# A gated MLP after sliding-window attention: the kept z pair's seven operand pieces made by GpSimd, through its own DMA queue

## The chip, the cores and the metric

The kernel runs on one core of a Trainium2 chip. The time is that of the device, in microseconds: 1127.86 us before the change, the median of three runs (1126.88 to 1131.13). Engines are called by the profile's names: PE is TensorE's matmul and PEld its weight load, DVE is VectorE, ACT is ScalarE, POOL is GpSimd, SP is SyncE, and a q behind the name (SPq) is the engine's queue of instructions, where DMAs are issued.

## The reference, cut to what matters

One block of a transformer on 2048 rows of 640 columns: a sliding-window attention (32 heads of 20, window 256) with its residual, and a gated MLP. The change lies in the second part:

```python
z  = gelu(layernorm(h) @ w_in)                                  # 2048 x 1728
z1 = z[..., :864]
z2 = layernorm(z[..., 864:])                                    # 2048 x 864
g  = einsum("ts,sf->tf", w_sp, z2) + b_sp[:, None]              # 2048 x 2048 by 2048 x 864
h2 = h + (z1 * g) @ w_out
```

The product with `w_sp` is the gate.

## The kernel before, in words

All matrix products are done in float32 pieces: each operand is split into a rounded high part (hi) and the rest (lo = raw - hi), and three products (hi hi, hi lo, lo hi) are summed in PSUM.

The gate cuts the 16 row tiles of z2 into pairs (tile k and tile k + 4, or k + 8 and k + 12), and uses a scheme of seven block products in place of eight. For each pair, the two tiles of 864 columns are four blocks of 432 columns (b11, b12 from one tile, b21, b22 from the other), and the right operand of the seven products are the seven pieces B11, T1 = b12 - b11, T2 = b22 - T1, B22, T3 = b22 - b12, B21 and T4 = b21 - T2, each as hi and lo. They lie in `zc[k]`, seven tiles of 128 x 2 x 432 for each of four k (named ze and zl in the profile). The sum over s is cut in halves. The opening half (`first_gate(p)`, p = 0 to 7) uses the z2 tiles 0 to 7 and stores its partial result to DRAM (`g_d`). Then `z2_pair` makes the other pairs, whose pieces overwrite `zc`, and `second_gate(p)` does the second half, loads the partial result, gates, and projects by `w_out`.

The first pair of the second half (tiles 8 and 12, `z2_pair(12, 8, 12, 0, True)`) is made ahead, before the opening half, when the four sets of `zc` are still full. This is the kept z pair. In the kernel before, DVE forms the raw pieces in place in the pair's two row buffers, with four subtractions between the stores: SP stores b11, b21, b22, T1, T3, T2, T4 to `z2_d`, each 128 x 432 (216 KB). Then `staged_pieces` takes one piece after the other through one SBUF tile, `stage` (128 x 2 x 432): SP loads the raw piece into `stage[:, 1]`, ACT rounds it into `stage[:, 0]` (hi), DVE subtracts in place to get lo, and SP stores both halves to `zp_d[m]` (432 KB). When PE has used a set of `zc[0]` for the last time, SP loads the finished pieces from `zp_d` (`ze<-zp_d`).

Each engine executes its instructions in order. In the attention part the order on PE, DVE and ACT is as written (`manual_schedule`). From there on, a scheduler of the tile framework puts the instructions of all engines in order, by its own simulated times, from the program order of the steps: `steps` is the list of products, and `at(n, f)` puts f in front of step n. `run(n)` emits both. A gate pair is seven steps of 12 matmuls of 128 x 432 (L1086).

For the gate's left operand, SP loads two tiles of `w_sp` per pair p into `fx` (two halves that take turns, L1036). ACT and DVE make seven pieces from them in `aw`: `copy` (ACT, L719) for hi, `minus` (DVE, L713) for lo and for the block sums, the one with two inputs in `tmp1` and `fx`. The posts of each step take PSUM to the row buffers: `copy` on ACT or `plus` on DVE (`row<-g`). There are four row buffers of 128 x 864. SP stores each finished row to `g_d` (L1099, L1100). A `copy` or `minus` has the helper's line (L719, L713) whatever it works on, so the tile names tell them apart.

Two more users of the same places: `e1["h"][0]`, the home of four raw tiles of `w_out` (`load_wout`, L1193, `stage<-w_out_in`) and later of h, is `stage` too. And POOL has nothing to do in the opening half of the gate.

## Time and profile before

| | |
|---|---|
| median of three runs | 1127.86 us (1126.88 to 1131.13) |
| profiled execution: its time, its span | 1126.43 us, 1124.6 us |
| mean granted TensorE clock in it | 0.997 |
| PE busy | 1090.6 us, 97% of the span |
| DVE, ACT, POOL busy | 719.1, 576.7, 307.4 us |
| opening half of the gate on PE | 697.85 to 838.10 us, 672 matmuls |
| staging of the kept pair (`stage` as its tile) | first load issued at 709.04 us, last store at 760.02 us |

The profile is one execution. Its views are: busy time by engine, groups of instructions by line and tile (count, busy time, mean length in ns, idle time of the engine just before them and what ended it), waits by who waited for whom, the timeline, the chain of work that ended last, and the table by stretches (busy time and count on each engine between two moments). Moments are counted from the start of the span.

### The profile page before, as it was taken

How to read it: one execution, taken by the hardware profiler on the slowest of the kernel's cores; microseconds unless marked ns; L12 is line 12 of the kernel's file. 1: busy time of each engine (PE TensorE's matmuls, PEld its weight loads, DVE VectorE, ACT ScalarE, POOL GpSimd, SP SyncE). 2: the span in 40 equal slices, each digit the busy share in tenths (PEclk: the TensorE clock that was granted, in tenths of full speed). 3: DMA queues.
4: the chain of work that ended last, by engine and by line, in shares of the span. 5: the costliest groups of instructions: out<-in, count | busy, mean ns of one | idle time of the engine just before them, and what ended most of it. 6: DMA issues, size and time to landing. Idle time of an engine off the chain costs nothing.

```text
span 1124.6 us, 27720 instructions
## 1 busy us (share of the span) xinstructions
PE 1090.6 (97%) x10667; PEld 976.9 (87%) x10667; DVE 719.1 (64%) x2049; ACT 576.7 (51%) x1228; POOL 307.4 (27%) x454
## 2 busy tenths in 40 slices
PE   8999999999999999989899999999999999999998
PEld 7998877668888776879899999889989899999998
DVE  6541113889999997687376578555547884556442
ACT  4334333259999999566666567333336521222210
POOL 3114444457777778311100254000002000000000
PEclk9999999999999999999999999999999999999999
DMA  7212665656666653688564511654371563344331
GB/s 258 77 31 100 174 213 175 207 199 200 205 214 205 203 166 122 199 277 271 208 194 161 166 54 40 200 179 166 124 256 40 177 211 118 125 148 147 99 95 59
DMA packets 88036, 181.78 MB, mean 162 GB/s; under 512 B 11536, under 2 KB 49680, under 8 KB 83984
## 3 DMA queue, kind: packets, MB, share of 16 engines
q1 hardware_dynamic: 85600, 174.76, 48.2%
q10 hardware_dynamic: 2304, 5.24, 1.2%
q8 instruction: 84, 1.38, 0.5%
q14 instruction: 48, 0.39, 0.1%
HBM read 118.65 MB, written 62.51 MB: 161 GB/s over the span
## 4 chain that ended last, share of the span: by engine, by line
PE 71%; DMA 9%; DVE 7%; issue 4%; POOL 3%; ACT 3%; SPq 2%; POOLq 0%; ACTq 0%; DVEq 0%
PE g L1086 18%; PE out_ps L1125 8%; PE pv L431 6%; PE bank L403 5%; PE bank L337 5%; PE zb L950 4%; PE zx L898 3%; PE zv L898 2%; PE qk L521 2%; PE qk L523 2%; PE qk L522 2%; DMA fx<-hn_d 2%; PE zy L898 2%; POOL sg L540 2%; DMA fx<-wsp_in 1%
## 5 line engine op out<-in xcount | busy, mean ns | idle before, releaser
L406 ACT ACTIVATE pt<-bank 128x384 f32<-128x384 f32 (+2 forms) x512 | 200.3, 492 | 11.8 <-PE bank L403 8.1
L719 ACT ACTIVATE aw<-fx 128x512 fp32r<-128x512 f32 (+2 forms) x160 | 93.0, 594 | 158.9 <-PE g L1086 91.0
L1086 PE MATMUL g<-zl,aw 128*128 128x432 f32 x768 | 171.9, 359 | 1.3 <-ACT zl L719 1.2
L349 DVE CUSTOM_DVE_ANT_0 junk<-bank,strip 128x288 bf16<-128x288 f32 x392 | 157.6, 454 | 2.6 <-PE bank L337 1.1
L1086 PEld LDWEIGHTS g<-zl,aw 128*128 128x128 f32 x768 | 143.6, 188 | 8.7 <-ACT zl L719 1.9
L1086 PE MATMUL g<-ze,aw 128*128 128x432 f32 x576 | 135.8, 363 | 6.0 <-DVE row L713 4.2
L431 PE MATMUL pv<-pt,v_sb 128*32 128x192 f32 (+3 forms) x1984 | 126.5, 321 | 2.5 <-POOL pt L411 1.8
L1086 PEld LDWEIGHTS g<-ze,aw 128*128 128x128 f32 x576 | 106.3, 188 | 14.6 <-ACT aw L719 5.5
L713 DVE TENSOR_TENSOR aw<-fx,aw 128x512 fp32r<-128x512 f32 (+2 forms) x152 | 96.9, 646 | 27.7 <-ACT aw L719 26.0
L403 PE MATMUL bank<-slot 123*32 123x288 bf16 (+5 forms) x1536 | 105.9, 280 | 3.1 <-issue 2.2
L1125 PE MATMUL out_ps<-wout,y_sp 128*128 128x320 f32 (+1 forms) x630 | 96.5, 309 | 0.4 <-ACT y_sp L135 0.4
L408 POOL TENSOR_SCALAR_AFFINE_SELECT pt<-pt 128x512 f32<-128x512 f32 x128 | 82.7, 647 | 47.1 <-ACT pt L406 46.1
L950 PE MATMUL zb<-win,aw 128*128 128x432 f32 x480 | 95.5, 359 | 0.0
L1125 PEld LDWEIGHTS out_ps<-wout,y_sp 128*128 128x128 f32 (+1 forms) x630 | 94.3, 188 | 1.2 <-ACT y_sp L135 0.7
L950 PEld LDWEIGHTS zb<-win,aw 128*128 128x128 f32 x480 | 89.9, 188 | 4.9 <-DVE aw L713 0.4
L337 PE MATMUL bank<-slot 120*32 120x288 bf16 (+2 forms) x1264 | 89.0, 283 | 1.1 <-DVE mcol L349 1.0
L537 DVE TENSOR_TENSOR rest<-qk,sg 128x512 f32<-128x512 f32 x40 | 27.7, 691 | 86.2 <-ACT sg L535 82.0
L411 POOL TENSOR_SCALAR_AFFINE_SELECT pt<-pt 128x512 f32<-128x512 f32 x112 | 73.7, 658 | 0.0
L713 POOL TENSOR_TENSOR aw<-fx,aw 128x640 fp32r<-128x640 f32 x8 | 13.5, 1692 | 217.2 <-ACT aw L719 217.2
L403 PEld LDWEIGHTS <-slot 123*32 123x32 bf16 x1536 | 52.7, 96 | 18.3 <-issue 7.4
L431 PEld LDWEIGHTS pv<-pt,v_sb 128*32 128x32 f32 x1984 | 59.5, 110 | 7.5 <-POOL pt L411 3.8
L540 POOL TENSOR_TENSOR sg<-rest,sg 128x512 bf16<-128x512 f32 x40 | 46.6, 1166 | 69.2 <-ACT sg L539 63.5
(193 smaller groups left out, 2172.7 us busy)
## 6 DMA issues: line engine op xcount, KB each, us to landing
fx<-wsp_in SPq DMA_DIRECT2D x32, 512.0 KB
slot<-qk_d SPq DMA_DIRECT2D x72, 200.0 KB
qk_d<-sg SPq DMA_DIRECT2D x32, 384.0 KB
slot<-qk_d SPq DMA_DIRECT2D x72, 160.0 KB
fx<-hn_d SPq DMA_DIRECT2D x32, 320.0 KB
o_d<-ot SPq DMA_DIRECT2D x64, 128.0 KB
z_d<-row SPq DMA_DIRECT2D x16, 432.0 KB
g_d<-row SPq DMA_DIRECT2D x16, 432.0 KB
```

Of the source, the lines that this page charges most:

```text
L337: nc.tensor.matmul(ps[32 * j:32 * j + 32, :n], part(st, half, 120, 0, hh, q0, 32), part(st, half, 120, 1, hh, lo + skip * j, n), start=Tru ...
L349: nc.vector.tensor_tensor_reduce(out=junk[:, :n], in0=ps[:, :n], in1=keep, scale=1.0, scalar=NEG, op0=OP.add, op1=OP.max, accum_out=m_cols ...
L403: nc.tensor.matmul(ps[32 * i:32 * i + 32, b:e], part(st, half, 123, 1, hh, k0, 32), part(st, half, 123, 0, hh, kb * P + b, e - b), start=T ...
L406: nc.scalar.activation(pt[:, hh, :n], ps[:, :n], AF.Exp, scale=SCALE)
L408: nc.gpsimd.affine_select(out=pt[:, :, :P], in_=pt[:, :, :P], pattern=[[0, 4], [1, P]], base=0, channel_multiplier=-1, compare_op=OP.is_ge ...
L431: nc.tensor.matmul(ps[32 * hh:32 * hh + 32, a - 512 * c:b - 512 * c], v_sb[:, kb, v0:v0 + 32], pt[:, hh, a - kb * P:b - kb * P], start=fir ...
L713: (eng or nc.vector).tensor_tensor(out=out, in0=a, in1=b, op=op)
L719: nc.scalar.activation(out, a, AF.Copy)
L898: nc.tensor.matmul(ps, a[x], b[:, y], start=start and m + x + y == 0, stop=stop and m == n - 1 and x == 1, skip_group_check=True)
L950: nc.tensor.matmul(b[0][:, :HF], a[t][:, x, kk], win2[0][:, y, kk, h * HF:(h + 1) * HF], start=kk + x + y == 0, stop=kk == KD - 1 and x == 1)
L1086: nc.tensor.matmul(ps, w[m][x][:, k], zc[k][m][:, y], start=start and k + x + y == 0, stop=stop and k == 3 and x == 1, skip_group_check=True)
L1125: nc.tensor.matmul(ps[j][:, :HD], src[:w, a, k, :], e1["wout"][:w, b, k, j * HD:(j + 1) * HD], start=(k == 0 and a + b == 0), stop=(k == K ...
```

## The change

The two tiles of the kept pair are stored whole and once (`z2_d` is now two tiles of 128 x 864), right after they are normalized. The four subtractions on DVE in the row buffers are gone. Everything after that is GpSimd's: for each piece it loads the block (and, for T1 to T4, the block or kept sum that is subtracted, into the place of hi), subtracts, stores the sums T1 and T2 - which T2 and T4 need - to a new DRAM tensor `t_d`, makes hi with a `tensor_copy` and lo with a subtraction, and stores both to `zp_d`. All these DMAs are issued in GpSimd's own queue. The pieces come in another order (B11, T1, B21, T2, B22, T3, T4); the loads of `zp_d` into `zc` stay on SP, and in their old order.

```diff
-    z2_d = dram.tile([7, P, HF], F32, name="z2_d")
+    z2_d = dram.tile([2, P, FH], F32, name="z2_d")
+    t_d = dram.tile([2, P, HF], F32, name="t_d")
...
-            b11, b12, b21, b22 = blocks
-
-            def keep(m, raw):
-                nc.sync.dma_start(z2_d[m], raw)
-
-            at(n0 + 4, lambda: keep(B11, b11))
-            at(n0 + 5, lambda: (keep(B21, b21), keep(B22, b22)))
-            at(n0 + 7, lambda: (minus(b11, b12, b11), minus(b12, b22, b12)))
-            at(n0 + 8, lambda: (keep(T1, b11), keep(T3, b12)))
-            at(n0 + 9, lambda: minus(b11, b22, b11))
-            at(n0 + 10, lambda: (keep(T2, b11), minus(b21, b21, b11)))
-            at(n0 + 11, lambda: keep(T4, b21))
+            for t in range(2):
+                at(n0 + 4 + t, lambda t=t: nc.sync.dma_start(z2_d[t], z[t]))
             return
...
     def staged_pieces(n0, n1):
-        raw = stage.bitcast(F32)[:, 1]
+        hi, raw = (stage.bitcast(F32)[:, k] for k in range(2))
+        eng = nc.gpsimd
+        b11, b12, b21, b22 = (z2_d[t, :, h * HF:(h + 1) * HF] for t in range(2) for h in range(2))
+
+        def piece(m, src, less=None, keep=None):
+            eng.dma_start(raw, src)
+            if less is not None:
+                eng.dma_start(hi, less)
+                minus(raw, raw, hi, eng)
+            if keep is not None:
+                eng.dma_start(keep, raw)
+            eng.tensor_copy(out=stage[:, 0], in_=raw)
+            minus(stage[:, 1], raw, hi, eng)
+            eng.dma_start(zp_d[m], stage.bitcast(F32))
+
+        for i, p in enumerate(((B11, b11), (T1, b12, b11, t_d[0]), (B21, b21), (T2, b22, t_d[0], t_d[1]), (B22, b22),
+                               (T3, b22, b12), (T4, b21, t_d[1]))):
+            at(n0 + 6 * i, lambda p=p: piece(*p))
         for i, m in enumerate((B11, T1, T2, B22, T3, B21, T4)):
-            n = n0 + 6 * i
-            at(n, lambda m=m: nc.sync.dma_start(raw, z2_d[m]))
-            at(n + 2, lambda: copy(stage[:, 0], raw))
-            at(n + 3, lambda: minus(stage[:, 1], raw, stage[:, 0].bitcast(F32)))
-            at(n + 4, lambda m=m: nc.sync.dma_start(zp_d[m], stage.bitcast(F32)))
             at(n1 + i + 1, lambda m=m: nc.sync.dma_start(zc[0][m].bitcast(F32), zp_d[m]))
...
-    staged_pieces(len(steps) + 8, len(steps) + 49)
+    staged_pieces(len(steps) + 4, len(steps) + 49)
```

What the scheduler makes of it is seen at three places. The first is POOL's order at the start of the gate's opening half (`mvz` is the column of layernorm statistics; `z_d` stands for `z2_d`, since numbers are cut from names). Before, the next work behind the last `mvz` belongs to the z pairs after the opening half:

```order
L976 TENSOR_TENSOR mvz_0_11692<-mvz_0_11692,half 128x1
L976 TENSOR_TENSOR mvz_1_11738<-mvz_1_11738,half 128x1
L713 TENSOR_TENSOR aw<-fx,aw 128x640 x2
```

With the change, the seven pieces stand between these two, of which the first two (B11, then T1) are:

```order
L977 TENSOR_TENSOR mvz_1_11739<-mvz_1_11739,half 128x1
L1004 DMA stage<-z_d 128x432
L1010 CAST stage<-stage 128x432
L714 TENSOR_TENSOR stage<-stage 128x432
L1012 DMA zp_d<-stage 128x864
L1004 DMA stage<-z_d 128x432
L1006 DMA stage<-z_d 128x432
L714 TENSOR_TENSOR stage<-stage 128x432
L1009 DMA t_d<-stage 128x432
L1010 CAST stage<-stage 128x432
L714 TENSOR_TENSOR stage<-stage 128x432
L1012 DMA zp_d<-stage 128x864
```

In all, POOL gains 20 DMAs, 7 casts and 11 subtractions there. The second place is ACT's order in the first pairs of the gate (`row<-g` takes a product out of PSUM, `aw<-fx` is a left operand's hi). Before:

```order
L719 ACTIVATE row_9611<-g_0_0_0_11767 128x432
L719 ACTIVATE stage<-stage 128x432
L719 ACTIVATE aw<-fx 128x512
L719 ACTIVATE row_9609<-g_1_0_0_11894 128x432
L719 ACTIVATE stage<-stage 128x432
L719 ACTIVATE aw<-fx 128x512
L719 ACTIVATE aw<-tmp_9614 128x512
L719 ACTIVATE row_9610<-g_1_1_1_11913 128x432
L719 ACTIVATE aw<-fx 128x512
L719 ACTIVATE stage<-stage 128x432
L719 ACTIVATE aw<-fx 128x512 x2
```

and now:

```order
L720 ACTIVATE row_9612<-g_0_0_0_11768 128x432
L720 ACTIVATE aw<-fx 128x512
L720 ACTIVATE row_9610<-g_1_0_0_11890 128x432
L720 ACTIVATE aw<-fx 128x512
L720 ACTIVATE aw<-tmp_9615 128x512
L720 ACTIVATE row_9611<-g_1_1_1_11908 128x432
L720 ACTIVATE aw<-fx 128x512 x3
```

The rest of ACT's order is the same without the `stage` rows, and DVE's is likewise: the seven `stage<-stage` subtractions and the four in the row buffers are out, the others keep their order (but for one neighbouring pair). On PE the same matmuls stand in the same order, but for a few groups of one to three in pairs 1 to 4, where the scheduler lets the products of two pairs alternate. The third place is SP's queue, at the first load of `w_out` into `stage`. Before, it stood behind the last `zp_d` store and the fifth `g_d` store of the opening half:

```order
L1011 DMA stage<-z_d 128x432
L1014 DMA zp_d<-stage 128x864
L1099 DMA g_d<-row_9611 128x864
L1193 DMA stage<-w_out_in 128x640
L1036 DMA fx<-wsp_in 128x1024
L1100 DMA g_d<-row_9612 128x864
```

and now it stands behind the tenth:

```order
L1103 DMA g_d<-row_9613 128x864
L1039 DMA fx<-wsp_in 128x1024
L1102 DMA g_d<-row_9612 128x864
L1196 DMA stage<-w_out_in 128x640
L1039 DMA fx<-wsp_in 128x1024
L1103 DMA g_d<-row_9611 128x864
```

Behind it there are the same stores and `w_sp` loads as before, and then the `ze<-zp_d` loads. From SP's queue 19 DMAs are gone: seven stores of raw pieces have become two of whole tiles, and seven loads and seven stores of `stage` are POOL's now.

## The prediction

> **What bounds the kernel now.** I read the busy times first: PE is busy for 97% of the span, so only PE's idle time can be won. Then I asked the stretch table for the gate's products alone (columns: stretch, its length, busy time and count on PE and on PEld, granted clock, share and rate of DMA).
>
> ```profile
> PE 1090.6 (97%) x10667; PEld 976.9 (87%) x10667; DVE 719.1 (64%) x2049; ACT 576.7 (51%) x1228; POOL 307.4 (27%) x454
> 697.85:760.62 62.77, 58.20 (x288) 53.33 (x288) 1.00 0.51 171
> 760.62:829.60 68.98, 68.65 (x348) 65.25 (x348) 1.00 0.49 157
> 829.60:838.10 8.50, 7.61 (x36) 6.61 (x36) 1.00 0.96 306
> ```
>
> The opening half is cut where the staging of the kept pair ends. Behind it, 348 matmuls take 68.98 us with 0.33 idle: 68.65 / 348 = 0.197 us each. At that pace the 288 matmuls ahead of it need 56.8 us; they took 62.77. So 6.0 us are lost while the staging runs. The clock is 1.00 in both, so it isn't that. The timeline of PE names the places (start, duration, what; in brackets the idle time before it and who ended it):
>
> ```profile
> 715.88 0.87 PE L1086 MATMUL g<-ze,aw 128*128 128x432 f32 x3 [1.37 <-DVE row L713]
> 726.25 0.66 PE L1086 MATMUL g<-ze,aw 128*128 128x432 f32 x2 [1.05 <-ACT aw L719]
> 753.36 0.86 PE L1086 MATMUL g<-ze,aw 128*128 128x432 f32 x3 [0.20 <-DVE row L713]
> 760.66 1.41 PE L1086 MATMUL g<-ze,aw 128*128 128x432 f32 x6 [1.93 <-DVE row L713]
> ```
>
> They sum to 4.55 us; the other 1.4 or so is the slow restart (3 matmuls in 0.86 us instead of 0.59) and some shorter gaps. Who is late shows on ACT and DVE:
>
> ```profile
> 716.28 0.53 ACT L719 ACTIVATE row<-g 128x432 f32<-128x432 f32 x1 [3.44 <-DMA z_d<-row]
> 725.11 0.56 ACT L719 ACTIVATE stage<-stage 128x432 fp32r<-128x432 f32 x1 [4.35 <-DMA stage<-z_d]
> 758.79 0.56 ACT L719 ACTIVATE stage<-stage 128x432 fp32r<-128x432 f32 x1 [4.76 <-DMA stage<-z_d]
> 759.39 0.61 DVE L713 TENSOR_TENSOR stage<-stage 128x432 fp32r<-128x432 f32 x1 [3.25 <-ACT stage L719]
> 759.91 0.60 DVE L713 TENSOR_TENSOR row<-g,row 128x432 f32<-128x432 f32 x1
> ```
>
> ACT reaches a hi of the kept pair, waits 4 to 5 us for its load, and DVE then waits for ACT; the PSUM sum of 759.91, which PE needs at 760.66, stands behind both. The stall of 726.25 is an `aw` hi behind the same wait on ACT. At 716.28 ACT waits for a row buffer that is being stored as a raw piece, while DVE makes T1, T3 and T2 in these buffers. From 700 to 770 us the groups are (count, busy time, mean ns, idle time ahead), and the third row is one of the four subtractions in the row buffers:
>
> ```profile
> L719 ACT ACTIVATE stage<-stage 128x432 fp32r<-128x432 f32 x7 | 4.0, 564 | 20.5 <-DMA stage<-z_d 20.5
> L713 DVE TENSOR_TENSOR stage<-stage 128x432 fp32r<-128x432 f32 x7 | 4.2, 605 | 12.2 <-ACT stage L719 12.2
> 713.58 0.61 DVE L713 TENSOR_TENSOR row<-row,row 128x432 f32<-128x432 f32 x1
> ```
>
> **The change part by part.** *Removed from ACT and DVE.* ACT loses 4.0 us of work and 20.5 of waiting, DVE 4.2 + 4 x 0.6 = 6.6 us and 12.2 of waiting. All three causes of the four stalls go with it, since the two tiles are stored at once and free their rows. Without them the 288 matmuls should run as the next 348 do, whose ACT and DVE have the same gate work: minus 6.0 us on PE's path. What follows the opening half hangs on PE and shifts with it; the 8.50 - 36 x 0.197 = 1.4 us lost behind 829.60 have no `stage` in them and stay.
>
> *SP* issues 19 fewer DMAs and has no `zp_d` store to wait with. SP's own time is not on the path, so this counts nothing by itself; the cover is that the `w_sp` loads are in time behind 760.62 as well, under the same rules.
>
> *Added to POOL.* Its work costs nothing while it ends before POOL or its results are wanted: POOL idled 133.63 us up to 838.87. The results are wanted earlier, by the `ze<-zp_d` loads and, ahead of these, by `stage<-w_out_in`, which now follows the tenth `g_d` store:
>
> ```profile
> 838.87 1.57 POOL L713 TENSOR_TENSOR aw<-fx,aw 128x640 fp32r<-128x640 f32 x1 [133.63 <-ACT aw L719]
> 704.67 4.35 DMA z_d<-row
> 709.04 2.69 DMA stage<-z_d
> 712.98 2.41 DMA zp_d<-stage
> 721.87 3.13 DMA stage<-z_d
> 794.33 0.33 SPq L1099 DMA_DIRECT2D g_d<-row  x1
> 797.58 0.33 SPq L1036 DMA_DIRECT2D fx<-wsp_in  x1
> 801.35 0.69 DVE L713 TENSOR_TENSOR fx<-fx 128x512 f32<-128x512 f32 x1 [1.43 <-DMA fx<-wsp_in]
> 801.35 1.15 ACT L719 ACTIVATE aw<-fx 128x512 fp32r<-128x512 f32 x2 [1.74 <-DMA fx<-wsp_in]
> ```
>
> The four DMA rows are from the chain of waits, the others from the timeline. Shifted by 6.0, SP comes to that load at 788.3, and the `w_sp` load behind it is wanted at 791.6. If POOL is not done then, the `w_sp` load is late, and ACT and DVE start on it the moment it lands: there is next to no slack. So POOL's chain has from about 709.3 (the whole tile's store takes the 4.35 us of the half tile's, a little more with twice the bytes) to 791.6: **82 us**.
>
> How long is it? Within a piece every step waits for the one before, since raw and lo share a place. Prices from rows (the slowest load of the staging, and POOL's groups over the whole span):
>
> ```profile
> 729.08 0.32 SPq L1011 DMA_DIRECT2D stage<-z_d  x1
> 734.76 0.56 ACT L719 ACTIVATE stage<-stage 128x432 fp32r<-128x432 f32 x1 [1.83 <-DMA stage<-z_d]
> L713 POOL TENSOR_TENSOR row<-row,row 128x432 f32<-128x432 f32 x6 | 8.1, 1344 | 7.2 <-DVE row L713 3.4 <-ACT row L982 1.5 <-DVE zl L713 1.1
> L408 POOL TENSOR_SCALAR_AFFINE_SELECT pt<-pt 128x512 f32<-128x512 f32 x128 | 82.7, 647 | 47.1 <-ACT pt L406 46.1
> L360 POOL CAST m<-mr 128x40 bf16<-128x40 f32 (+1 forms) x16 | 4.0, 249 | 1.0
> L976 POOL TENSOR_TENSOR mvz<-mvz,half 128x1 f32<-128x1 f32 x16 | 10.1, 631 | 44.6 <-DVE mvz L975 44.6
> ```
>
> A subtraction is 1.3 us. A cast of 432 columns lies between 0.25 (40 columns) and 1.34; I take 0.6, from the one-input operation on 512 columns. A load of 216 KB is 2.7 us and a 432 KB store 2.4 when SP issues them. No row shows a DMA issued by GpSimd. Below, it costs what SP's does (0.3 us of issue, inside these times). Above, each takes the slowest that this stage shows, 4.35 us for a store and 5.7 for a load (issued at 729.08, used at 734.76). I add 0.6 us per DMA, because even the smallest POOL instruction takes 0.63. Then a plain piece (B11, B21, B22) is 3.3 + 0.6 + 1.3 + 3.0 = 8.2 us; T3 and T4 have a second load issued behind the first (0.6) and a subtraction more, 10.1; T1 and T2 also wait for the kept sum's store (3.0, of which 0.6 lie under the cast), 12.5. In all 3 x 8.2 + 2 x 10.1 + 2 x 12.5 = 70 us, ending at 779. The lower bound is 58 (20 x 0.6 less), ending at 767; the upper, with 7 loads 2.4 dearer, 9 stores 1.4 dearer and 7 casts 0.7 dearer, 104, ending at 813. I take 70: 12 us to spare, or 0.6 us more for each of the 20 DMAs.
>
> The Trainium skill ("DMA: Bandwidth & Descriptors", Specifications) gives the first byte of a DMA from GpSimd as about 1 us, against 0.6 from SP. By that the surcharge is 0.4 us per DMA, and the estimate of the chain 66 us instead of 70: the same verdict.
>
> *POOL beside DVE.* What POOL does at the same time as DVE is not free for DVE. Before the gate, between 600 and 700 us, where POOL works on the z pairs, DVE's subtractions are longer than in the gate:
>
> ```profile
> L713 DVE TENSOR_TENSOR ze<-row,ze 128x432 fp32r<-128x432 f32 x9 | 8.1, 906 | 1.8 <-ACT ze L719 1.8
> L713 DVE TENSOR_TENSOR zl<-row,zl 128x432 fp32r<-128x432 f32 x11 | 8.5, 795 | 0.1
> L713 DVE TENSOR_TENSOR row<-g,row 128x432 f32<-128x432 f32 x9 | 5.3, 599 | 0.0
> 657.03 1.55 POOL L713 TENSOR_TENSOR row<-row,row 128x432 f32<-128x432 f32 x1 [1.53 <-ACT row L982]
> 658.55 1.93 POOL L713 TENSOR_TENSOR aw<-fx,aw 128x640 fp32r<-128x640 f32 x1
> 658.07 2.87 DVE L713 TENSOR_TENSOR ze<-row,ze 128x432 fp32r<-128x432 f32 x2 [0.47 <-ACT ze L719]
> 660.00:680.00 20.00, 20.00 (x104) 19.04 (x103) 15.07 (x32) 13.42 (x23) 13.30 (x13) 1.00 0.20 60
> ```
>
> The first two rows are from that stretch, the third from the gate between 700 and 770. Two DVE subtractions beside POOL took 2.87 us instead of 1.2. By the first two groups, 20 operations were stretched by 9 x 0.31 + 11 x 0.20 = 4.9 us, beside 12 POOL subtractions of this size, 16 us. POOL now brings 11 subtractions and 7 casts, 18.5 us, into the gate: some 5.7 us more on DVE, less than the 6.6 taken off it. It costs where a PSUM sum stands behind a stretched operation: PE gives it one step, 12 x 0.197 = 2.4 us, of which 0.6 is the sum itself, so a single hit of about 1 us passes and two in a row do not. I put it at 1.0 us on PE (three or four short stalls with their restarts); below 0, above the whole 6.0.
>
> **The sum.** 1126.4 (the profiled execution: span 1124.6 and 1.8 around it) - 6.0 + 1.0 = 1121.4. The median shown lies 1.4 above the profiled one, so 1121.4 + 1.4 is about **1122.6**, 0.5% less than 1127.86 (0.47%). A difference under 0.5%, 5.6 us, is about what a measurement of this kernel can't tell from none; the forecast lies on that edge.
>
> **The rivals.**
>
> *A. The forecast*, 1120.4 to 1124.6: chance 0.60. At the low end POOL costs DVE nothing that PE sees and the median lies no higher than the profiled execution, at the high end it costs three times my 1.0.
>
> *B. POOL's reads give the stalls back.* DVE's chain (sum of blocks, lo, PSUM sum) is hit twice in a row, several times in the five pairs under POOL's chain. For it: the rows above, and that POOL's casts and subtractions stand back to back, 1.9 us. Against: from 660 to 680 us (last row above: PE, PEld, DVE, ACT, POOL) DVE was busy for 15.07 of 20 us, POOL for 13.30, and PE without a gap. Price: 3 to 6 us back, so 1125 to 1128: chance 0.14. The Trainium skill speaks for this rival ("SBUF — State Buffer", Who interferes with whom): a DVE instruction with two SBUF inputs and a GpSimd instruction that reads SBUF exclude each other, and the later one waits for the whole of the earlier. The 2.87 us agree with it.
>
> *C. POOL's chain outlasts its time.* Slower than before. Place: SP waits at `stage<-w_out_in`, with the `w_sp` loads of pairs 6 and 7 and two `g_d` stores behind it. Up to 82 us it costs nothing, then PE loses a microsecond for each; from about 87 us the gain is gone, from 93 on the kernel is over 0.5% slower. With 95 us: 1122.6 + 13 = 1135.6. For it: the upper bound of 104 and that no row has a DMA of GpSimd's. Against: the four 2.4 and 2.7 us transfers were this short in the same stage. Chance 0.16, of which 0.14 ends slower by over 0.5%.
>
> *D. The loads of `w_sp` were the true cause.* In the chain of waits, two of them take over 6 us in this stage:
>
> ```profile
> 727.87 6.27 DMA fx<-wsp_in
> 744.67 6.73 DMA fx<-wsp_in
> ```
>
> The change moves 6.7 MB instead of 6.05 (loads and stores of 216 and 432 KB) through the same 16 DMA engines, so these stay as slow, and half of the gain is missed: 1125.6: chance 0.10. Against it: DVE and ACT also wait for `w_sp` behind 760.62 (801.35), and PE does not stall. What the change takes away is waits in ACT's and DVE's order, not transfers. The Trainium skill speaks for this rival too ("DMA: Bandwidth & Descriptors", Issuing engines are not separate DMA queues): DMAs issued by several engines run on the same DMA engines, and only issue time is saved; no row here shows two queues at once in this stage.
>
> **How the numbers follow.** Faster by over 0.5% is the lower half of A and a little more: 0.38. Within 0.5%: the rest of A, B, D and the mild end of C: 0.48. Slower: C, 0.14. The range for 8 in 10 runs from 1119.8 (A's low end, with 0.6 for the measurement) to 1130, which leaves out most of C.
>
> **What would show it.** Right: no `stage` group on ACT and DVE before 838, 288 matmuls of the gate in 57 to 58.5 us, POOL's last `zp_d` store landed by about 780 (58 to 82 us after the first load), and SP's wait at `stage<-w_out_in` short. B would show as DVE subtractions of 0.9 us and more in the gate, with PE's idle times ended by `row`. C would show as a POOL chain past 791, an SP wait there and ACT waiting for `fx<-wsp_in` around 795. D would leave PE's idle times at the same places, with DVE and ACT waiting for `fx<-wsp_in`. The forecast is wrong if the opening half takes over 138 us or under 133.

## The result and the profile after

The changed kernel takes 1121.78 us (median of 20 runs, 1117.61 to 1128.23), the kernel before 1127.15 us beside it (20 runs, 1123.01 to 1133.81). The ratio is 0.9948 (95% interval 0.993 to 0.9965): 5.4 us less, some 0.8 us below the forecast of 1122.6.

The lines that answer to those shown of before come from the profiled execution of the changed kernel. Its span is long, 1126.5 us. The same kernel, run again, was profiled at 1116.7 us. Of the 9.8 us between the two, 6.1 lie ahead of the gate, whose first product comes at 701.48 us in the one and at 695.34 in the other (694.8 to 701.5 in all the executions profiled here, whatever the kernel). The other 3.9 lie in the opening half: a stall of 2.54 us, shown below, and a stretch of lower clock (0.95 granted from 806 to 840 us, worth 0.05 x 34 = 1.7 us). The busy times of its page, then three rows of its stretch table (columns as before): the opening half, the stretch with the lower clock, and the stretch that was cut out before:

```profile
PE 1093.3 (97%) x10667; PEld 979.0 (87%) x10667; DVE 718.4 (64%) x2038; ACT 575.9 (51%) x1221; POOL 336.8 (30%) x492
701.48:839.89 138.41, 134.59 (x673) 127.24 (x672) 76.57 (x121) 51.91 (x93) 31.78 (x40) 0.99 0.54 178
806.00:840.00 34.00, 32.90 (x157) 30.70 (x158) 16.21 (x27) 11.51 (x20) 0.00 (x0) 0.95 0.65 199
701.35:760.62 59.27, 59.27 (x304) 56.66 (x303) 37.86 (x63) 25.70 (x47) 18.18 (x24) 1.00 0.50 165
```

PE is now busy without a gap where before it lost 6.0 us: 304 matmuls in 59.27 us, 0.195 us each. The repeated execution shows the whole opening half without the low clock, from its first matmul to the first of the next part, ahead of the same stretch of before:

```profile
695.34:829.87 134.53, 132.97 (x674) 125.77 (x672) 76.59 (x121) 51.81 (x93) 31.12 (x40) 1.00 0.55 185
```

```profile
697.86:837.85 139.99, 134.30 (x673) 125.37 (x672) 77.50 (x132) 54.36 (x100) 1.48 (x2) 1.00 0.52 172
```

That is 5.5 us less at the same clock, about what the medians differ by: the gain lies in this half. The four stalls of PE have gone; the timeline of PE between 690 and 850 us in the profiled execution of after has a short and a long new one, and the two of the end, 0.40 and 0.70 us, which were there before:

```profile
793.76 1.42 PE L1089 MATMUL g<-ze,aw 128*128 128x432 f32 x6 [0.18 <-DVE row L714]
805.95 0.86 PE L1089 MATMUL g<-ze,aw 128*128 128x432 f32 x3 [2.54 <-DVE row L714]
```

The stall of 2.54 us is the place that the prediction named for rival C. Timeline of after, POOL, SP, ACT and DVE (the q behind SP is its queue):

```profile
713.33 0.76 POOL L1004 DMA_DIRECT2D stage<-z_d  x1 [4.59 <-DMA z_d<-row]
...
795.49 0.56 POOL L1012 DMA_DIRECT2D zp_d<-stage  x1 [0.30 <-POOL stage L714]
798.38 0.33 SPq L1196 DMA_DIRECT2D stage<-w_out_in  x1
798.81 0.38 SPq L1039 DMA_DIRECT2D fx<-wsp_in  x1
804.02 0.69 DVE L714 TENSOR_TENSOR fx<-fx 128x512 f32<-128x512 f32 x1 [5.29 <-DMA fx<-wsp_in]
804.02 1.15 ACT L720 ACTIVATE aw<-fx 128x512 fp32r<-128x512 f32 x2 [5.59 <-DMA fx<-wsp_in]
SPq L1196 <- DMA zp_d<-stage: 4.2, 1, 4.2
```

POOL's chain began at 713.33 and its last store landed at about 798.2: 85 us. The last row, from the waits of SP (in total, times, longest), says that SP stood 4.2 us at the `w_out` load. The `w_sp` load behind it was issued at 798.81 and landed at 804.02, and PE lost 2.54 us. In the repeated execution SP waited there 1.4 us, and PE has no stall that follows from it: the `w_sp` load was issued 1.6 us earlier, counted from the first gate matmul (95.7 instead of 97.3), and landed after 4.2 us instead of 5.2.

### The profile page after: what moved, and what is told of

Its sections match the earlier page's. It is cut to its first block, busy times and chain, and to the rows that moved or that the text cites. A ratio compares the mean times of both kernels' runs of the same rounds, so it can differ in the third digit from the quotient of the medians.

```text
span 1126.5 us, 27720 instructions
## 1 busy us (share of the span) xinstructions
PE 1093.3 (97%) x10667; PEld 979.0 (87%) x10667; DVE 718.4 (64%) x2038; ACT 575.9 (51%) x1221; POOL 336.8 (30%) x492
## 4 chain that ended last, share of the span: by engine, by line
PE 70%; DMA 12%; POOL 4%; DVE 4%; issue 4%; SPq 3%; ACT 2%; POOLq 0%; DVEq 0%; ACTq 0%
PE g L1089 14%; PE out_ps L1128 8%; PE zb L951 7%; PE pv L432 6%; PE bank L404 5%; PE bank L338 5%; PE zx L899 3%; DMA zp_d<-stage 2%; PE zv L899 2%; PE qk L522 2%; PE qk L524 2%; PE qk L523 2%; PE zy L899 2%; DMA fx<-hn_d 2%; DMA stage<-z_d 2%
## 5 line engine op out<-in xcount | busy, mean ns | idle before, releaser
L714 DVE TENSOR_TENSOR aw<-fx,aw 128x512 fp32r<-128x512 f32 (+2 forms) x152 | 100.2, 669 | 29.9 <-ACT aw L720 28.2
L714 DVE TENSOR_TENSOR row<-g,row 128x432 f32<-128x432 f32 x80 | 48.1, 603 | 30.0 <-PE g L1089 26.8
```

The lines of the kernel that those rows point to most:

```text
L714: (eng or nc.vector).tensor_tensor(out=out, in0=a, in1=b, op=op)
```

## The experiments

"Opening half" below is the time between the first gate matmul and the first `zb` matmul behind it, of one profiled execution. "w_sp" are three moments, counted from the first gate matmul, at which the first `w_sp` load of the fourth, fifth and sixth gate pair was issued (from the timeline, on whichever queue it is). Medians are shown as the difference to the kernel before, run beside it; the ratio is an estimate of its own and not that of the medians.

| run | ratio (95% interval) | median, us | opening half, us | w_sp, us |
|---|---|---|---|---|
| before | 1 | 0 | 139.99 | 29.1, 45.9, 65.1 |
| the change, again | 0.9942 (0.992 to 0.9965) | -6.3 | 134.53 | 22.4, 39.5, 57.2 |
| w_out load on POOL | 0.9949 (0.9929 to 0.9968) | -5.6 | 133.64 | 22.4, 39.5, 57.2 |
| the same, in a later comparison | 0.9964 (0.9943 to 0.9985) | -4.7 | 134.98 | 22.4, 39.5, 57.2 |
| no staging work | 0.9934 (0.9915 to 0.9953) | -7.0 | 133.68 | 22.4, 39.5, 57.2 |
| staging DMAs on POOL only | 0.9947 (0.9931 to 0.9963) | -5.2 | 135.85 | 26.9, 43.7, 57.8 |
| staging compute on POOL only | 0.999 (0.9969 to 1.001) | -1.5 | 136.78 | 27.3, 41.7, 60.0 |
| staging stores on POOL only | 0.9984 (0.9964 to 1.0004) | -1.3 | 138.25 | 26.2, 42.6, 61.2 |
| staging loads on POOL only | 0.9985 (0.9966 to 1.0005) | -1.6 | 136.81 | 25.1, 43.9, 60.9 |
| w_sp loads on POOL only | 0.9984 (0.9965 to 1.0002) | -2.7 | 136.11 | 26.7, 42.7, 60.7 |
| 14 more reads on POOL | 0.9961 (0.9941 to 0.9981) | -3.3 | 139.07 | 23.2, 39.6, 57.5 |
| longer chain | 0.9953 (0.9935 to 0.9971) | -5.8 | 133.97 | 22.4, 39.5, 57.7 |
| longer chain, w_out load on POOL | 0.9949 (0.9933 to 0.9966) | -5.6 | 134.08 | 22.4, 39.5, 57.4 |

The granted clock is 1.00 in all these opening halves but that of "14 more reads", where it was 0.66 from 805 to 810 us, some 1.7 us of its 139.07. One kernel, the `w_out` load on POOL, was profiled twice, at 133.64 and 134.98 us: differences of up to 1.3 us between single executions mean nothing. And the moments of "w_sp" hold PE's own losses too: by 65.1 in the kernel before, PE had itself lost nearly 6 us.

One caution goes with all of them. The scheduler puts every kernel's engines in order anew, so a run that changes one thing in the program usually changes some places in the orders of PE, DVE and ACT as well. Only the pairs said to have equal orders are free of that.

### What POOL's chain costs: the w_out load, and the reads

The first run is the change unaltered. The second gives the first `w_out` load to POOL, so that SP never waits for the chain; the orders of PE, DVE and ACT are those of the change.

> The changed kernel once more, beside the others. Theory: the opening half of the gate loses no more than 0.5 us on PE up to the wait of SP at the first w_out load, then 2 to 3 us behind it, because the w_sp load that follows in SP's queue is late; ratio to before 0.993 to 0.997. Rival (that wait was an accident of the one profiled execution, whose chain on GpSimd happened to be long): the chain from first load to last store landed takes 70 to 78 us here instead of 85, SP does not wait, PE loses nothing there.

```diff
-                nc.sync.dma_start(wout_raw(k), w_out[k * P:(k + 1) * P, :])
+                (nc.sync if k else nc.gpsimd).dma_start(wout_raw(k), w_out[k * P:(k + 1) * P, :])
```

> The changed kernel with one DMA moved: the first load of w_out into the staging tile is issued by GpSimd, behind its chain, instead of by SP. The order on PE, DVE and ACT is the same. Theory (SP's wait there is what the change gives back): the 2.5 us stall of PE around 806 is gone and the time is 2 to 3.5 us below the changed kernel's, 1118 to 1120. Rival (the w_sp load is late anyway, by its own buffer or by the DMA engines): PE stalls there as before, no difference to the changed kernel.

> The changed kernel with the first w_out load issued by GpSimd, a second time, beside the longer chains: 1120.5 to 1121.8, the foot for their comparison. Rival C would have the longer chain with that load on SP 3 to 7 us above it, the other theory within 1.5 us.

SP's wait at this load is gone, and no time can be told apart: -5.6 and -4.7 us beside -6.3. The 2 to 3.5 us that I expected did not come; the stall that they were to remove had not come back in the repeated execution either, whose chain took 83 us. What SP waits for POOL therefore costs at most 2 to 3 us, which is about what these intervals resolve.

The third run leaves the staging out: no loads, casts, subtractions or stores of pieces, and the z tiles as they are go into `zc[0]`, so the output is not the reference's.

```diff
...
-        for i, p in enumerate(((B11, b11), (T1, b12, b11, t_d[0]), (B21, b21), (T2, b22, t_d[0], t_d[1]), (B22, b22),
-                               (T3, b22, b12), (T4, b21, t_d[1]))):
-            at(n0 + 6 * i, lambda p=p: piece(*p))
...
-            at(n1 + i + 1, lambda m=m: nc.sync.dma_start(zc[0][m].bitcast(F32), zp_d[m]))
+            at(n1 + i + 1, lambda m=m: nc.sync.dma_start(zc[0][m].bitcast(F32), z2_d[m % 2].rearrange("p (a n) -> p a n", a=2)))
```

> The changed kernel without any staging: the two tiles of the kept pair are stored, but no piece of them is made, and the seven tiles of the second half's first set are loaded from the stored tiles as they are. This leaves out the 20 DMAs, 7 casts and 11 subtractions on GpSimd (the result is that of other operands). It is what the opening half costs with nothing beside it. Theory (the staging's waits cost 6.0 us before, GpSimd's work beside DVE costs nothing that PE sees): 288 of its matmuls take 56.8 us, and the time is within 1 us of the one with the w_out load moved, 5.5 to 6.5 below before. Rival (GpSimd's reads and transfers cost PE something in the changed kernel all along): 2 us and more below that one.

Its opening half is 133.68 us, with POOL idle; with the whole chain on POOL and the `w_out` load out of SP's way it is 133.64. The rows of the two stretches (no staging work; then the `w_out` load on POOL):

```profile
697.69:831.37 133.68, 132.59 (x673) 126.00 (x672) 72.36 (x121) 52.04 (x93) 1.47 (x2) 1.00 0.41 138
```

```profile
695.81:829.45 133.64, 132.55 (x673) 126.00 (x672) 75.85 (x122) 52.13 (x93) 32.53 (x41) 1.00 0.55 186
```

POOL has 31 us more, DVE 3.5 us more, PE the same to 0.04 us. That close an agreement is chance: the second execution of the kernel with the `w_out` load on POOL took 134.98 us, and most of the difference is one stall of PE behind a subtraction of DVE's that lasted 1.51 us beside one of POOL's (0.69 in the repeated execution of the change). POOL, DVE and PE there:

```profile
791.28 1.13 POOL L714 TENSOR_TENSOR stage<-stage 128x432 fp32r<-128x432 f32 x1
791.44 1.51 DVE L714 TENSOR_TENSOR tmp<-fx 128x512 f32<-128x512 f32 x1 [4.64 <-DMA fx<-wsp_in]
793.62 1.42 PE L1089 MATMUL g<-ze,aw 128*128 128x432 f32 x6 [1.09 <-DVE row L714]
```

So the chain as built costs PE between nothing and some 1 us; what is left to win beyond the change is at most what lies between -6.3 and -7.0, inside the intervals.

### Whose wait was it: ACT's and DVE's order, or SP's queue

The prediction put the lost 6.0 us down to ACT and DVE standing in their order at staging work, and gave SP's 19 fewer DMAs no value. The next run is the kernel before with only the DMAs of the staging moved to POOL's queue; ACT and DVE still compute.

```diff
-            at(n, lambda m=m: nc.sync.dma_start(raw, z2_d[m]))
+            at(n, lambda m=m: nc.gpsimd.dma_start(raw, z2_d[m]))
...
-            at(n + 4, lambda m=m: nc.sync.dma_start(zp_d[m], stage.bitcast(F32)))
+            at(n + 4, lambda m=m: nc.gpsimd.dma_start(zp_d[m], stage.bitcast(F32)))
```

> The kernel before with one part of the change: the seven loads and seven stores of the staging tile are issued by GpSimd, but ACT makes hi and DVE lo, and the five-step making of raw pieces on DVE and their stores stay as before. Theory (the stalls come from ACT and DVE waiting in their order for the staging loads): they wait as before or longer, since a DMA from GpSimd takes some 0.6 us more; PE loses 5 to 8 us up to the end of the staging; time within 0.3% of before. Rival (the stalls come from SP's queue, in which the staging's loads and stores hold up the w_sp loads): most of the 6 us is won, ratio 0.995 to 0.997.

It gained 5.2 us in the medians, nearly all (4.1 us in the profiled opening half), where I had expected nothing. ACT still waited 17.4 us (20.5 before) for `stage` loads in its order, and PE kept the stall at the row buffers:

```profile
L719 ACT ACTIVATE stage<-stage 128x432 fp32r<-128x432 f32 x7 | 4.0, 565 | 17.4 <-DMA stage<-z_d 17.4
715.25 0.86 PE L1086 MATMUL g<-ze,aw 128*128 128x432 f32 x3 [1.42 <-DVE row L713]
```

The counterpart is the changed kernel with all DMAs of the chain back on SP. POOL computes; ACT and DVE have no staging work at all.

```diff
         def piece(m, src, less=None, keep=None):
-            eng.dma_start(raw, src)
+            nc.sync.dma_start(raw, src)
...
-            eng.dma_start(zp_d[m], stage.bitcast(F32))
+            nc.sync.dma_start(zp_d[m], stage.bitcast(F32))
```

> The changed kernel, but all DMAs of the kept pair's chain (loads, kept sums, stores) are issued by SP again; GpSimd keeps the casts and subtractions, ACT and DVE have none of it. Theory ORDER (the prediction's: the 6 us were lost because ACT and DVE stood in their order at work on the kept pair): these waits are gone here too, so the gain stays, 1120.5 to 1122.5 (ratio 0.994 to 0.996), with SP waiting in its queue and nobody feeling it. Theory QUEUE (SP's queue, where w_sp loads stood behind staging DMAs that waited for their turn, is where the 6 us came from): SP now waits some 50 us for POOL and for landings between w_sp loads, these land as late as before or later, and the time is 1125.5 to 1132 (ratio 0.999 to 1.005), with PE's idle times ended by aw or by DVE's rows and ACT and DVE waiting for w_sp.

The ratio is 0.999 (0.9969 to 1.001), against 0.9942 (0.992 to 0.9965) with these DMAs on POOL. The two intervals do not overlap, and neither kernel has staging work in ACT's or DVE's order: with ACT and DVE free, it matters whose queue holds these DMAs. Freeing ACT and DVE alone brings a part at most, up to 3.5 us by the interval (3.2 us in the profiled opening half). It isn't their value alone that is measured, though, since SP is held longer here than before (35.8 us at the stores instead of 28.1). SP's waits and timeline, and ACT, DVE and PE in this run:

```profile
SPq L1012 <- POOL stage L714: 35.8, 7, 9.0
724.39 0.32 SPq L1012 DMA_DIRECT2D zp_d<-stage  x1
725.28 1.65 SPq L1039 DMA_DIRECT2D fx<-wsp_in  x2
730.95 1.15 ACT L720 ACTIVATE aw<-fx 128x512 fp32r<-128x512 f32 x2 [5.93 <-DMA fx<-wsp_in]
734.74 0.86 PE L1089 MATMUL g<-ze,aw 128*128 128x432 f32 x3 [1.06 <-DVE row L714]
751.50 0.86 PE L1089 MATMUL g<-ze,aw 128*128 128x432 f32 x3 [1.54 <-DVE row L714]
```

SP waits 35.8 us for POOL before the seven stores, and the two `w_sp` loads of a pair stand behind one of them. They are issued 27.3 us after the first gate matmul instead of 22.4, and ACT then waits 5.93 us for the first. DVE's PSUM sum comes late behind that, and PE waits for it (734.74). So in this run a queue that holds waiting DMAs stalls PE, through loads that have nothing to do with what it waits for.

Could one half of the staging DMAs be enough? Two runs take only the stores, or only the loads, off SP (the two lines of the diff above, one at a time).

> The kernel before, with only the seven stores of finished pieces issued by GpSimd; SP keeps their loads, ACT and DVE keep the computing. In the kernel before SP waited 28.1 us at these stores. Theory QUEUE: that wait is gone from SP, but each load now waits in SP's queue for the store before it, some 20 us in all, so part of the gain: 1122.5 to 1125.5 (ratio 0.996 to 0.999). Theory ORDER: nothing, ACT and DVE wait as before: 1126 to 1128. Third possibility: what gained in the run with all staging DMAs on GpSimd was the scheduler's later places for ACT's and DVE's staging work; then this run, whose order on ACT is moved likewise, gains the whole 5 us (1121 to 1122.5), with SP still waiting 15 us or more at the staging loads.

> The kernel before, with only the seven loads of raw pieces issued by GpSimd; SP keeps the stores of finished pieces, ACT and DVE the computing. Theory QUEUE: SP still stands at the stores until DVE has made lo, 20 to 30 us in all, with w_sp loads behind: little or no gain, 1125 to 1128 (ratio 0.998 to 1.001). Theory ORDER: nothing, 1126 to 1128. If the scheduler's other order was the gain of the run with all staging DMAs on GpSimd: 1121 to 1123, with SP still waiting 20 us or more.

Neither can be told from the kernel before by its median (their profiled opening halves are 1.7 and 3.2 us shorter). With the stores away, SP waits at the loads, since a load needs the place that the store before it reads; with the loads away, SP waits at the stores. Rows of SP's waits, stores on POOL first, then loads on POOL:

```profile
SPq L1011 <- DMA zp_d<-stage: 24.7, 6, 7.9
```

```profile
SPq L1014 <- DVE stage L713: 34.0, 6, 10.2
```

They do not settle whether the scheduler's other order was part of the gain. In the traces, the seventh `stage` operation of ACT stands behind 31 of its gate operations (`row<-g` and `aw`, from its first `row<-g`) in the kernel before, behind 36 and 38 in these two runs, and behind 41 in the run with all staging DMAs on POOL. So the order was moved there by 10 places, and here by 5 and 7. Later places in ACT's and DVE's order remain a rival for a part of that run's 5.2 us.

The next run leaves all staging where it was and takes the `w_sp` loads out of SP's queue:

```diff
-                nc.sync.dma_start(view(fx, f0 + o, 8, P), wsp[t, :, 8 * c:8 * c + 8, :])
+                (nc.gpsimd if p and not c else nc.sync).dma_start(view(fx, f0 + o, 8, P), wsp[t, :, 8 * c:8 * c + 8, :])
```

> The kernel before, with one thing changed: in the gate's opening half the w_sp loads of pairs 1 to 7 are issued by GpSimd, which is idle there. All staging of the kept pair stays on SP, ACT and DVE. Theory QUEUE: the w_sp loads no longer stand behind staging DMAs, so they are issued some 7 us earlier (22 to 23 us and 39 to 40 us behind the first gate matmul, as with the change) and most of the gain comes: 1121 to 1123 (ratio 0.994 to 0.997), though ACT and DVE still wait 15 to 20 us and some 10 us at the staging tile. Theory ORDER: these waits in ACT's and DVE's order stay, and so does the time: 1126 to 1128 (ratio 0.999 to 1.001). If both are needed: about half, 1123.5 to 1125.

About half came in the medians, -2.7 us, and the opening half of the profiled execution is 3.9 us shorter; but the ratio, 0.9984 (0.9965 to 1.0002), does not exclude that nothing came. The loads were still late (26.7, 42.7, 60.7), though no staging DMA stood ahead of them in POOL's queue. What they waited for is in POOL's waits and timeline, with what ran on ACT and DVE just before the second load of the fourth pair (its first, at 723.96, waited for DVE's `aw` too):

```profile
POOL fx L1036 <- DVE aw L713: 79.5, 9, 19.0
L719 ACT ACTIVATE stage<-stage 128x432 fp32r<-128x432 f32 x7 | 4.0, 566 | 17.2 <-DMA stage<-z_d 17.2
724.97 0.57 ACT L719 ACTIVATE stage<-stage 128x432 fp32r<-128x432 f32 x1 [2.03 <-DMA stage<-z_d]
725.57 0.61 DVE L713 TENSOR_TENSOR stage<-stage 128x432 fp32r<-128x432 f32 x1 [1.91 <-ACT stage L719]
727.08 0.54 POOL L1036 DMA_DIRECT2D fx<-wsp_in  x1 [2.54 <-DVE aw L713]
```

A `w_sp` load overwrites a half of `fx`, so it also needs DVE to be done with that half, and DVE was held up at the staging tile, in its order. A `w_sp` load therefore needs two things: a free place, which ACT's and DVE's staging delayed, and its turn in the queue, which SP's staging DMAs delayed. Only the kernels with neither delay reach 22.4, 39.5 and 57.2. How the 6 us divide between the two stays open: the runs of each alone give 1.5 to 5.2 us in the medians and 3.2 to 4.1 us in the profiled opening half (the two half measures left aside), these overlap in effect, and each run has an order of its own. Nor do late loads explain everything: with only the staging DMAs on POOL the first two moments are as late as with the `w_sp` loads there (26.9 and 43.7), and PE does not stall behind them.

### Two times the reads, and a longer chain

Two additions of POOL behind each piece's store, in what was waiting time, into a tile that nobody reads (the `w_out` load on POOL, as above):

```diff
             eng.dma_start(zp_d[m], stage.bitcast(F32))
+            for _ in range(2):
+                plus(pad, hi, raw, eng=eng)
```

> The changed kernel with the first load of w_out issued by GpSimd, and two more additions of GpSimd behind each piece's store (14 in all, 128x432, two SBUF operands, into a tile that nobody reads): some 19 us more of reading beside DVE in the gate's opening half, in what was waiting time. Rival B of the prediction (GpSimd's reads hold up DVE and PE feels it): at my price of 1.0 us for 18.5 us, 1.0 us more; at B's price 3 to 6 us more, 1124 to 1127. Theory FREE (DVE's operations get 0.1 to 0.2 us longer, and PE does not wait for DVE there): as the kernel with that load on GpSimd, 1120.5 to 1121.8, with PE busy 158 to 159 of the 160 us from 690 to 850.

1123.5 us, ratio 0.9961: between the two theories, and not told apart by the intervals from the same kernel without the additions (0.9949 and 0.9964). The trace, however, shows the mechanism of rival B. A group of DVE's between 705 and 800 us, then the timeline of DVE, PE and SP:

```profile
L714 DVE TENSOR_TENSOR aw<-fx,aw 128x512 fp32r<-128x512 f32 x32 | 30.7, 977 | 9.0 <-ACT aw L720 9.0
794.29 3.59 DVE L714 TENSOR_TENSOR aw<-fx,aw 128x512 fp32r<-128x512 f32 x2
797.94 1.05 PE L1092 MATMUL g<-ze,aw 128*128 128x432 f32 x4 [1.69 <-DVE aw L714]
797.91 0.33 SPq L1042 DMA_DIRECT2D fx<-wsp_in  x1
805.13 0.95 PE L1092 MATMUL g<-ze,aw 128*128 128x432 f32 x3 [1.81 <-DVE row L714]
```

Two of DVE's operations took 3.59 us beside POOL's reads; PE waited for the second, and the next `w_sp` load waited for DVE to be done with `fx`, which made the second stall. These are 3.5 us of stalls, where the two executions without the additions have none and 1.09 us. PE's and DVE's orders differ in places between the two kernels, so the size is not exact.

The last pair makes the chain longer by a subtraction per piece, whose result is overwritten. In one the `w_out` load is SP's, in the other POOL's; their orders of PE, DVE and ACT are equal.

```diff
+            minus(hi, raw, raw, eng)
             eng.tensor_copy(out=stage[:, 0], in_=raw)
```

> The changed kernel with one subtraction more per piece (into hi's place, before hi is made; the result is overwritten and the output is the same): GpSimd's chain is 7 x 1.4 = 10 us longer, ending some 95 us after its first load instead of 83 to 85. The first w_out load stays on SP, where the scheduler puts it one w_sp load later. Rival C of the prediction (each microsecond of the chain past its time costs one): 4 to 8 us more than the changed kernel, 1125 to 1129, with an SP wait of 5 to 10 us at that load. Theory LATER PLACE (the scheduler knows the chain's length and lets SP come to the load later, so the wait stays short): 1120.5 to 1122.5, with an SP wait under 3 us.

> As the run with the longer chain, but the first w_out load is issued by GpSimd behind its chain, so SP never waits for the chain; the orders of PE, DVE and ACT are the same in these two. Rival C: the cost is SP's wait, so this run is back at 1120.5 to 1122, 3 to 7 us under the other. Theory LATER PLACE: no difference between the two (under 1.5 us), both at 1120.5 to 1122.5; what both have over the changed kernel, if anything, comes of GpSimd's 7 more reads beside DVE (0 to 1 us).

Both took what the change takes, and they differ by 0.2 us, though SP waited long in the first:

```profile
SPq L1197 <- DMA zp_d<-stage: 7.6, 1, 7.6
805.21 0.33 SPq L1040 DMA_DIRECT2D fx<-wsp_in  x1
```

The scheduler knew of the longer chain and let one more `w_sp` load pass ahead of the `w_out` load. The load behind it was issued 106.3 us after the first gate matmul (805.21 - 698.89), exactly as in the run where SP did not wait (804.03 - 697.71). So 7.6 us of waiting cost nothing there, where 4.2 us had cost 2.54. My expectation of 10 us more for the chain was too high as well: it took 87 us, 2 to 7 more than the others' 80 to 85.

## Why the prediction was right, and where it was not

**The size.** The prediction takes 6.0 us off and adds 1.0 back. Its sum has a slip: 1121.4 + 1.4 is 1122.8 and not 1122.6, so by its own terms it missed the median by 1.0 us. Measured: 5.5 us off the opening half in the repeated execution, 6.35 and 5.0 in the two where SP doesn't wait at `w_out`. By its own sign (wrong if the opening half takes over 138 us) the first profiled execution, 138.41 us, speaks against it; 2.54 us of that are the stall at the `w_out` load and some 1.7 the lower clock, and the repeated one, 134.53, lies inside. The pace that it took as the goal, 56.8 us for 288 matmuls, is what the change reached (288 x 0.195 = 56.2). That the stretch behind the staging shows the pace that remains when nobody is late, was the step that made the number right.

**The cause of the four stalls: half right.** The waits in ACT's and DVE's order were there, and all three causes went as forecast: no `stage` operation of ACT or DVE is left before 838 us, and PE's four stalls are gone. But the step "Without them the 288 matmuls should run as the next 348 do" fails if the DMAs stay with SP: with ACT and DVE freed alone, the ratio was 0.999, and PE had two stalls, of 1.06 and 1.54 us.

**"SP's own time is not on the path, so this counts nothing by itself": wrong.** This is the step that failed. Putting the chain's DMAs back on SP took most of the gain away in the medians, and taking only the DMAs from SP gave 5.2 us, with a changed order. The row was in the waits of before: SP waited 28.1 us before the stores, for DVE, with `w_sp` loads behind. SP's and ACT's timeline of before follow:

```profile
SPq L1014 <- DVE stage L713: 28.1, 7, 7.9
743.75 0.33 SPq L1036 DMA_DIRECT2D fx<-wsp_in  x1
751.42 0.63 ACT L719 ACTIVATE aw<-fx 128x512 fp32r<-128x512 f32 x1 [5.86 <-DMA fx<-wsp_in]
```

I counted SP's instructions and not what stood behind its waits. The longest stall of before shows how the two waits hang together. The fifth pair's first `w_sp` load was issued at 743.75, behind the `zp_d` store of 742.54. ACT waited 5.86 us for that pair's loads, so the next hi, lo and store came late, at 752.01, 753.22 and 753.85, and so did the load of the next piece, at 756.26, for which ACT waited 4.76 us ahead of PE's stall at 760.66. But the queue was not the last thing that held the load: it waited 0.8 us more for DVE to be done with its place, and DVE had waited 2.38 us for the hi of ACT. In the kernel before, turn and place come almost together, and so the run that gave the `w_sp` loads a free queue alone won little.

**Rival D** had the right object, the `w_sp` loads, and the wrong reason. They stayed as slow as it said: one issued at 744.67 before was there at 751.42, one issued at 777.94 with the change at 784.58, and PE did not stall. What changed is when they were issued. The lateness of the sixth pair's, 65.1 instead of 57.2, is mostly PE's own loss by then, and no stall follows from it, since PE has 0.33 us idle behind 760.62.

The Trainium skill ("DMA: Bandwidth & Descriptors", Issuing engines are not separate DMA queues) says that issuing from several engines saves only issue time. The change and the run with its DMAs back on SP, ratios 0.9942 and 0.999, do not agree: there SP also stood waiting in its queue, 35.8 us for POOL.

**POOL's chain: 70 us forecast, 80 to 85 measured.** The operations were priced well (cast 0.54 to 1.07 us, subtraction 1.11 to 1.62), and GpSimd's issue takes 0.55 us, against 0.32 for SP's. Two terms were too small. Ahead of a DMA that follows an operation of POOL's there are 0.30 us more (the row of 795.49). And the stores were long whenever `w_sp` loads had just been issued; I had taken the price of a quiet moment, 2.41 us. Timeline of after, POOL and SP:

```profile
769.03 0.56 POOL L1012 DMA_DIRECT2D zp_d<-stage  x1 [0.30 <-POOL stage L714]
772.03 0.55 POOL L1004 DMA_DIRECT2D stage<-z_d  x1 [2.44 <-DMA zp_d<-stage]
775.91 0.33 SPq L1039 DMA_DIRECT2D fx<-wsp_in  x1
777.94 0.38 SPq L1039 DMA_DIRECT2D fx<-wsp_in  x1
779.89 0.56 POOL L1012 DMA_DIRECT2D zp_d<-stage  x1 [0.30 <-POOL stage L714]
785.97 0.55 POOL L1004 DMA_DIRECT2D stage<-z_d  x1 [5.52 <-DMA zp_d<-stage]
```

From 769.03 a store takes 3.00 us until the next load is issued; from 779.89, 2 to 4 us behind two `w_sp` loads, 6.08. The bounds of 58 and 104 held it, but the last store landed at 798 and not by about 780, and the 12 us to spare did not exist.

**Rival C: the place right, the price wrong.** All three of its signs came in the profiled execution of after: a chain past 791, SP's wait, and ACT's wait for `w_sp`, until 804. SP did wait at `stage<-w_out_in`, and PE did stall behind it once. But of 4.2 us PE felt 2.54, of 1.4 and of 7.6 nothing: how much a wait costs there hangs on which `w_sp` load stands behind it, and the scheduler moves the load when the chain gets longer. "Up to 82 us it costs nothing, then PE loses a microsecond for each" assumed an order that stays.

**POOL beside DVE: 5.7 us on DVE forecast, 4.7 measured, and on PE 0 to 1.1 instead of 1.0.** DVE's groups of after between 705 and 800 us, and the same groups before:

```profile
L714 DVE TENSOR_TENSOR aw<-fx,aw 128x512 fp32r<-128x512 f32 x34 | 26.2, 786 | 9.4 <-ACT aw L720 9.3
L714 DVE TENSOR_TENSOR row<-g,row 128x432 f32<-128x432 f32 x15 | 9.0, 602 | 5.9 <-PE g L1089 5.9
L714 DVE TENSOR_TENSOR tmp<-fx 128x512 f32<-128x512 f32 x6 | 5.1, 844 | 14.2 <-DMA fx<-wsp_in 14.2
L714 DVE TENSOR_TENSOR fx<-tmp,fx 128x512 f32<-128x512 f32 x6 | 4.5, 755 | 0.1
```

```profile
L713 DVE TENSOR_TENSOR aw<-fx,aw 128x512 fp32r<-128x512 f32 x31 | 20.9, 686 | 6.9 <-ACT aw L719 6.7
L713 DVE TENSOR_TENSOR row<-g,row 128x432 f32<-128x432 f32 x15 | 8.9, 600 | 1.1 <-PE g L1086 1.1
L713 DVE TENSOR_TENSOR tmp<-fx 128x512 f32<-128x512 f32 x6 | 4.2, 692 | 14.6 <-DMA fx<-wsp_in 14.6
L713 DVE TENSOR_TENSOR fx<-tmp,fx 128x512 f32<-128x512 f32 x5 | 3.4, 685 | 0.0
```

34 x 0.10 + 6 x 0.15 + 6 x 0.07 is 4.7 us. (Over the whole opening half, against the run without staging work, it was 3.5 us.) The PSUM sums, which PE waits for, stayed at 600 ns. **Rival B**'s mechanism is real, then: with the staging's reads alone PE lost up to 1.09 us at one place in one execution and nothing in another, and with twice the reads it had 3.5 us of stalls. These are single executions, so no threshold follows from them.

The time came out right in part by luck. The change takes the staging off ACT and DVE and off SP's queue at once, so the step that gave SP's queue no value could not show in the time. And the two smaller terms came and went with the execution: 0 to 1.1 us for POOL's reads, where the sum had 1.0, and 0 to 2.5 us for the `w_out` load, where it had nothing.

## What to carry to other kernels

A queue of DMAs works in order, as these traces show: before giving its issues no value, look in its waits for the transfers that stand long for someone else, and ask which unrelated loads stand behind them. Then ask what would have held those loads anyway. When a load waits both for its place and for its turn, removing one of the two may bring only a part, so test them apart before naming the cause, and compare the orders that the scheduler made of the tests. Price a chain of transfers by the slow ones of its stage, those issued just behind other traffic, and not by the quiet ones.

## What the hardware showed that I had not expected

- A DMA issued by GpSimd occupies it for 0.55 us, and 0.30 us pass before it when it follows GpSimd's own operation. Issue to landing of the 432 KB stores was 2.7 to 5.8 us, the long ones where two 512 KB loads had been issued up to 4 us before.
- DVE's operations with both inputs in SBUF got longer beside POOL's reads (0.686 to 0.786 and, with twice the reads, 0.977 us), those with one input in PSUM not at all (0.600 and 0.602 us). The Trainium skill ("SBUF — State Buffer", Who interferes with whom) says so: outside its 2-port modes, a DVE instruction with at most one SBUF input does not contend with GpSimd. The 0.600 and 0.602 us agree.
- In one execution PE did not feel 3.5 us more on DVE within 134 us (133.64 and 133.68 us), though it waits for DVE's sums throughout the gate; in the next execution of the same kernel one subtraction stretched from 0.69 to 1.51 us came just ahead of a sum, and PE stood 1.09 us.
